# Decay attention with a mixture of experts on one core: constant rows by memsets, a new planned order, and transposes of the identity in TensorE's planned waits

## The chip, the cores and the metric

The kernel runs on one core of a Trainium2 chip. The metric is the device time of the whole program in microseconds (us), the median of three executions; lower is better. TensorE is called PE, VectorE DVE, ScalarE ACT, GpSimd POOL and SyncE SP, as in the profile.

## What is computed

For 8 batches and 8 heads of 576 rows with 64 columns each, in fp32, a causal attention whose scores carry a decay, and then a mixture of four experts over its output, each expert a causal attention of its own:

```python
scores = scale * (q @ k.T)
cum = cumsum(log(clip(f, 1e-4, 1)))
scores = where(causal, -1e9, scores + cum[:, None] - cum[None, :])
attn = softmax(scores) @ v                        # 8 batches x 8 heads
x = attn laid out as [8, 576, 512]
logits = x @ w_gate                               # 4 experts, the best 2 of each row count
for e in range(4):
    y = softmax(causal(scale * (x @ wq[e]) @ (x @ wk[e]).T)) @ (x @ wv[e]) @ wo[e]
    out += (weight of e in its row, 0 if not among the best 2) * y
```

## The kernel before

The work is cut into 48 units. A unit of kind a is two heads of one batch (4 for each batch, 32 in all); a unit of kind m is two experts of one batch (2 for each batch, 16 in all). The list `seq` starts with the four a units of batch 0; after that each batch's a units are followed by the m units of the batch before.

An a unit loads k and q of its two heads by four DMAs into a tile `nat` (L611, one of three buffers), turns them on PE (L624, 18 transposes of 64 columns, five chunks and then four, k on array rows 0 to 63 and q on rows 64 to 127), splits them into a rounded high part `kq` on ACT (L589) and a rest `ka` on DVE (L593), finds each row's maximum (PE L869, in the first two units also L872; DVE L888), turns the maxima (PE L925), copies them to `ms` (ACT L931) and moves them by DMA into one row of the tile `xa` (L399). The score matmuls (L965) end with one product of `xa` rows, which adds the decay and takes the maxima away. ACT makes the exponentials `P` (L976), POOL clears the diagonal (L982, L993), and PE multiplies with the values (L1038). DVE divides (L1085), PE turns the result back (L1101). From the third a unit on the maximum uses a table `tab` that POOL (L654) makes from the cumulated logs `cum`, which a DMA brings (L646). The m units project with the weights (L709, L827, L1165).

Tile `xa` (three buffers, 128 rows of 2 x 576 + 64 elements) holds per head, in rows 0 and 1 of its half, the two parts of the cumulated logs in the first 576 columns and constant -1 behind column 640; in row 63 the maxima, and -1 in the other columns of the first half. The function `consts` in `setup` fills it once: DVE or POOL writes -1 into the first 640 columns (L417), POOL zero into the others (L419), and then, for each half, the function `ones` issues a DMA (L424) that copies the -1 of rows 2 and 3 into rows 0 and 1 behind column 640. That is six DMAs in all. The rows of the cumulated logs come by L562 for the first unit and L568 for later ones.

What order the instructions have on each engine is worked out in Python while the kernel is built. Each piece of work is an `Op` with an engine, a key, a cost, the ops it depends on and the buffers it needs. `key` is the unit's number plus an offset by class of work (`PLAN`, by position in the batch, with `HEAD` and `TAIL` for the first and last four units). `Plan.run` goes through the ops by list scheduling: on each engine, among the ops that could start within `EPS` ns of the earliest one, that with the lowest key is taken. `Plan.start` says when an op can start by the model, `Plan.commit` books its cost: a PE op by its matmuls, a DMA by the time to issue it on SP, to land it and a `SLACK`. At the end every op's `emit` is called in the order of planned starts. Only the order reaches the chip; waits are real semaphores.

The planner's prices that the prediction uses: in `commit`, a DMA keeps SP for `issue` + 25 ns, goes at `t + issue + 450` or when the DMA before is through, takes `w` and lands `lat` later. In `dma`, a load of 576 packets of 256 bytes has `w` = 648 ns and `lat` = 1150 ns.

All loads and moves go through the one queue of SP.

Of the kernel before, what the change touches and what calls it, by code (L numbers as in the profile page):

```python
# [36 lines left out]
PLAN = dict(
    apply=((-3.69, -0.2), (1.91, 2.08), (-1.97, -2.51), (-2.59, -2.5), (2.97, 2.56), (-1.38, 0.57)),
    attend=((1.59, 6.1), (-1.72, 5.2), (1.87, 1.49), (1.87, 2.69), (2.89, 3.69), (2.85, 4.34)),
    cast=((-0.09, 1.61), (-1.47, 0.26), (-2.36, -1.76), (-2.3, -0.86), (-3.26, 1.5), (-6.95, -9.62)),  # L40
    front=((0.72, 3.77), (-4.95, 0.97), (-4.36, -7.02), (5.84, 9.48), (-1.56, 0.46), (-4.78, 0.96)),
    gate=((7.82, 17.49), (4.37, 7.38), (9.59, 17.28), (14.77, 14.75), (8.61, 13.31), (18.19, 18.71)),
    max=((-1.9, -1.68), (-3.57, -3.64), (-0.47, -0.46), (-1.25, -0.63), (-1.82, -0.88), (-1.83, -2.1)),
    mprep=((-5.49, -9.51), (-1.24, -8.56), (-2.91, -12.12), (-3.19, -8.05), (-3.1, -5.52), (-2.85, -5.41)),
    out=((12.37, 14.16), (-1.66, 5.19), (2.45, 9.19), (-5.4, 2.51), (1.88, 3.69), (5.94, 11.28)),
    prep=((-2.48, -0.56), (-2.12, -1.35), (-1.47, 0.32), (-1.82, -1.28), (-7.94, -3.61), (-8.41, -7.56)),
    rows=((-2.65, -6.62), (-11.0, -7.07), (-7.02, -3.23), (0.54, -3.2), (-6.33, -6.66), (-12.92, -13.93)),
    scores=((0.28, 0.67), (-1.44, -0.13), (-0.19, 0.25), (0.44, 0.37), (0.14, 0.03), (-0.76, 0.22)),
    sums=((-6.73, -12.09), (1.61, -9.24), (1.96, -8.53), (-4.38, -9.45), (-6.78, -10.99), (0.71, -7.59)),
    tabs=((5.21, -2.24), (1.53, -1.04), (6.91, 3.73), (5.35, -0.7), (4.67, 5.66), (-1.3, -5.57)),  # L50
    vals=((0.98, 0.65), (-0.3, -2.45), (-2.29, -5.3), (12.26, 9.3), (0.95, -0.58), (-7.18, -4.77)),
    weights=((6.93, 7.78), (16.12, 11.74), (9.43, 13.9), (4.47, 0.64), (15.35, 16.26), (9.04, 10.64)),
)
HEAD = dict(
    apply=(2.47, -1.78, -1.25, -2.7),
    attend=(-7.68, 3.1, -2.45, 6.22),
    cast=(-4.21, 0.81, 0.11, -0.52),
    front=(0.43, -1.73, 2.53, -4.04),
    gate=(0.37, -1.4, 0.8, -2.56),
    max=(-0.16, 0.86, -0.39, -1.35),  # L60
    mprep=(-2.19, -2.56, -2.41, 0.64),
    out=(-1.03, -4.48, -4.91, 0.66),
    prep=(-1.04, -0.44, -0.77, -1.26),
    rows=(-3.6, 3.37, -6.01, 0.74),
    scores=(0.31, 0.06, -0.21, -0.82),
    sums=(1.68, -3.76, 8.84, 0.33),
    tabs=(-2.41, 2.74, -1.74, 0.12),
    vals=(-0.52, 1.02, -3.29, -1.71),
    weights=(-0.08, 0.15, -5.46, -0.48),
)  # L70
TAIL = dict(
    apply=(-2.89, -2.65, 2.02, -6.52),
    attend=(3.47, 3.57, -4.81, 3.48),
    cast=(2.71, 0.37, 2.7, -1.07),
    front=(0.32, 1.1, -3.27, 0.54),
    gate=(-6.28, 1.66, -0.23, -2.38),
    max=(1.3, -3.61, -1.97, -1.97),
    mprep=(-2.15, -3.8, -7.38, 0.89),
    out=(-3.35, -4.26, 2.2, 1.98),
    prep=(0.41, -0.09, -0.26, -0.55),  # L80
    rows=(-0.23, 1.14, -2.46, -0.58),
    scores=(-2.96, -1.16, -0.35, 1.14),
    sums=(0.78, 4.91, -6.86, 2.75),
    tabs=(-0.79, -0.4, 2.07, 0.65),
    vals=(-3.77, -8.29, 4.81, 4.15),
    weights=(-6.29, -3.27, -0.84, 0.24),
)
# [53 lines left out]
class Plan:
# [1112 lines left out]
```

## Time and profile before

| | us |
|---|---|
| median of 3 runs | 670.53 |
| lowest and highest | 668.12, 671.59 |
| the profiled execution, its own time | 670.77 |
| the profiled execution, its span | 669.1 |
| PE busy in the span | 636.9 (95%) |
| DVE, ACT, POOL busy | 440.2, 333.6, 238.0 |

Times in views are us from the start of the span. The granted clock of PE is a share of full speed: 1.00 is 2.4 GHz, 0.50 is 1.2 GHz. A timeline's row is: start, duration of the run of equal instructions, engine, line, operation, out<-in, shape, count, and in brackets the idle time of the engine before it with what ended it. SPq stands for SP issuing DMAs: the duration is that of the issue, not of the transfer.

### The profile page before, as it was taken

The numbers are of one execution on the slowest core, as the hardware profiler recorded it, in microseconds if no ns is written. First come the engines' busy times: TensorE is split into PE (matmuls) and PEld (weight loads), VectorE is DVE, ScalarE is ACT, GpSimd is POOL, SyncE is SP. The second block draws the span as 40 slices with busy tenths as digits, with TensorE's granted clock in tenths as the row PEclk, the third lists the DMA queues.
The fourth block names the chain that finished last, engine by engine and source line by source line (L and its number), as shares of the span: only waits on it lengthen the run. The fifth ranks groups of instructions, "written<-read, shape, count | busy, mean of one in ns | idle before, by whom it ended". The sixth has DMA issues, their size and how long they took to land.

```text
span 669.1 us, 29785 instructions
## 1 busy us (share of the span) xinstructions
PE 636.9 (95%) x11928; PEld 611.5 (91%) x11928; DVE 440.2 (66%) x1889; ACT 333.6 (50%) x1092; POOL 238.0 (36%) x597
## 2 busy tenths in 40 slices
PE   3797899999999999999999999999999999999996
PEld 3586799989999999999999999999999999999995
DVE  4666467778578576776678775775677764753541
ACT  2443645564536643555436554566346544534543
POOL 6254566144324434144334434143332431100110
PEclk9887899999999999999999999999999999999999
DMA  4788686156412651256412662147622310001004
GB/s 99 139 170 166 135 157 132 47 128 107 87 38 67 169 122 40 54 119 170 102 38 58 147 134 57 40 102 175 112 58 55 105 38 21 3 18 65 3 6 140
DMA packets 136817, 60.62 MB, mean 91 GB/s; under 512 B 123260, under 2 KB 123740, under 8 KB 136680
## 3 DMA queue, kind: packets, MB, share of 16 engines
q1 hardware_dynamic: 136680, 58.73, 39.4%
q8 instruction: 93, 1.52, 1.0%
q14 instruction: 44, 0.36, 0.2%
HBM read 48.54 MB, written 9.88 MB: 87 GB/s over the span
## 4 chain that ended last, share of the span: by engine, by line
PE 80%; DMA 5%; ACT 4%; issue 4%; DVE 2%; POOL 2%; SPq 2%; POOLq 0%; ACTq 0%; DVEq 0%
PE ps L1038 22%; PE ps L965 20%; PE ps L827 15%; PE ps L709 9%; PE ps L869 5%; PE ps L1165 4%; DMA cum<-exn 2%; ACT P L976 2%; PE ps L624 2%; PE ps L1101 2%; DMA xa<-ms 1%; ACT xh L1137 1%; DMA out_dram<-outb 1%; DVE junk L888 1%; PE ps L925 1%
## 5 line engine op out<-in xcount | busy, mean ns | idle before, releaser
L976 ACT ACTIVATE P<-ps 128x320 f32<-128x320 f32 (+3 forms) x384 | 166.8, 492 | 36.8 <-PE ps L965 19.4
L654 POOL TENSOR_SCALAR_AFFINE_SELECT tab<-cum 128x192 f32<-128x192 f32 (+1 forms) x300 | 127.8, 452 | 75.5 <-DVE mxs L888 55.7
L888 DVE CUSTOM_DVE_ANT_0 junk<-ps,tab 128x64 bf16<-128x64 f32 (+2 forms) x300 | 119.6, 433 | 18.1 <-PE ps L869 10.8
L965 PE MATMUL ps<-kq,ka 64*128 64x320 f32 (+4 forms) x576 | 114.8, 323 | 1.2 <-DVE mxs L888 0.7
L593 DVE TENSOR_TENSOR ka<-ps,kq 128x320 fp32r<-128x320 f32 (+2 forms) x192 | 78.3, 451 | 53.3 <-ACT kq L589 53.1
L1038 PE MATMUL ps<-va,P 128*64 128x65 f32 x3400 | 111.5, 223 | 0.4 <-POOL tab L654 0.3
L1038 PEld LDWEIGHTS ps<-va,P 128*64 128x64 f32 x3400 | 106.9, 138 | 5.0 <-POOL tab L654 1.9
L965 PE MATMUL ps<-ka,kq 64*128 64x320 f32 (+4 forms) x576 | 106.7, 299 | 0.0
L965 PE MATMUL ps<-kq 64*128 64x320 f32 (+4 forms) x576 | 104.4, 297 | 0.2 <-issue 0.2
L982 POOL TENSOR_SCALAR_AFFINE_SELECT P<-P 128x256 f32<-128x256 f32 x96 | 39.1, 407 | 182.3 <-ACT P L976 172.9
L589 ACT ACTIVATE kq<-ps 128x320 fp32r<-128x320 f32 (+2 forms) x192 | 66.7, 411 | 60.6 <-PE ps L827 27.0
L993 POOL TENSOR_SCALAR_AFFINE_SELECT P<-P 128x256 f32<-128x256 f32 x96 | 39.0, 406 | 124.0 <-ACT P L976 120.3
L965 PEld LDWEIGHTS ps<-kq,ka 64*128 64x128 f32 (+1 forms) x576 | 73.5, 184 | 5.2 <-DVE mxs L888 1.5
L869 PE MATMUL ps<-kq 64*128 64x320 f32 (+4 forms) x576 | 75.7, 312 | 2.1 <-ACT kq L589 0.7
L965 PE MATMUL ps<-xa 64*128 64x320 f32 (+4 forms) x384 | 72.6, 302 | 4.9 <-DMA xa<-ms 4.9
L965 PEld LDWEIGHTS ps<-kq 64*128 64x128 f32 (+1 forms) x576 | 72.6, 183 | 0.7 <-issue 0.4
L965 PEld LDWEIGHTS ps<-ka,kq 64*128 64x128 f32 (+1 forms) x576 | 71.7, 183 | 0.2
L888 DVE CUSTOM_DVE_ANT_0 junk<-ps,mask 128x320 bf16<-128x320 f32 (+3 forms) x144 | 56.8, 420 | 16.8 <-ACT spot L546 8.1
L869 PEld LDWEIGHTS ps<-kq 64*128 64x128 f32 x576 | 56.7, 191 | 6.5 <-ACT kq L589 1.5
L965 PEld LDWEIGHTS ps<-xa 64*128 64x128 f32 (+1 forms) x384 | 52.1, 186 | 6.1 <-issue 4.3
L1065 DVE TENSOR_SCALAR rc<-ps 128x6 f32<-128x6 f32 x96 | 15.5, 162 | 57.5 <-PE ps L1038 57.5
L709 PE MATMUL ps<-vh,xh 64*128 64x260 f32 x320 | 52.7, 288 | 0.1
(127 smaller groups left out, 1553.2 us busy)
## 6 DMA issues: line engine op xcount, KB each, us to landing
cum<-exn SPq DMA_DIRECT2D x60, 288.0 KB
nat<-in_k_dram SPq DMA_DIRECT2D x64, 144.0 KB
nat<-in_q_dram SPq DMA_DIRECT2D x64, 144.0 KB
va<-in_v_dram SPq DMA_DIRECT2D x64, 128.0 KB
out_dram<-outb SPq DMA_DIRECT2D x24, 256.0 KB
out_dram<-nat SPq DMA_DIRECT2D x8, 256.0 KB
xa<-ms SPq DMA_DIRECT2D x64, 2.5 KB
va<-in_v_dram SPq DMA_DIRECT2D x32, 32.0 KB
```

The lines of the kernel that those rows point to most:

```text
L589: lambda: nc.scalar.activation(kqb.t[:, w, a:z], bank.t[:, :n], AF.Copy), [dep], [bank, kqb],
L593: lambda: nc.vector.tensor_tensor(kab.t[:, w, a:z], bank.t[:, :n], kqb.t[:, w, a:z].bitcast(F32), ALU.subtract),
L654: lambda cb=cb, tb=tb, i0=i0, o=o, n=n: nc.gpsimd.affine_select(tb.t[:, o : o + n], cb.t[:, :n], [[-1, n]], ALU.is_ge, NEG, base=i0, chann ...
L709: nc.tensor.matmul(banks[blk].t[:, :NV], xt[r, c0 : c0 + 128], (wl if i == 1 else wh)[r, c], start=(t == FIRST5[blk] and j == 0), stop=(j ...
L827: nc.tensor.matmul(banks[w][gg].t[:, :HS], (wl if i == 2 else wh)[r, c, es], x["l" if i == 1 else "h"][c].t[r, gg * HS : gg * HS + HS], st ...
L869: nc.tensor.matmul(banks[h].t[:, o:z], kf[:, S + i0 : S + i0 + 128], kf[:, j0 : j0 + n], start=True, stop=not decay)
L888: nc.vector.tensor_tensor_reduce(junk[turn[0] % 2][:, :n], bank.t[:, o:z], tab[h].t[:, at : at + n] if tab else mask[:, MW - n :], 1.0, lo ...
L965: nc.tensor.matmul(banks[h].t[:m, o:z], l, r, start=(i == 0), stop=(i == 3))
L976: lambda: nc.scalar.activation(pb.t[:, h, o : o + n], bank.t[:, :n], AF.Exp, scale=SCALE), [dep], [bank, pb],
L982: g.affine_select(pv, pv, [[0, 2], [1, 128]], ALU.is_ge, 0.0, base=0, channel_multiplier=-1)
L993: g.affine_select(pv, pv, [[0, 2], [1, 128]], ALU.is_ge, 0.0, base=0, channel_multiplier=-1)
L1038: nc.tensor.matmul(banks[s // 3].t[64 * c : 64 * c + 64, o : o + 65], lhs, vget(h, jb), start=jb == 0, stop=jb == t // 2)
```

## The change

1. The six DMAs of `ones` become six memsets of -1 on DVE, of two rows and 576 columns each, which wait for POOL's zeros in the same columns only.
2. All offsets in `PLAN`, `HEAD` and `TAIL` are new; a new table `SHIFT` adds an offset for each of the 48 units to each of the 15 classes. `EPS` shrinks on ACT, POOL and SP, `SLACK` grows a little, the planner's price for issuing a load becomes 650 ns for 576 packets, 1100 for 1024, 560 for 512 and 470 for others, where it was 510 for all. The memsets of `pads` get key 2.5 instead of 1.0.
3. Where a PE op takes a new PSUM bank, starts before 100 us of planned time and the plan has PE idle for more than 500 ns before it, `commit` notes a fill: (idle - 200) / 58 rounds of one transpose of the identity for each of at most two of the op's new banks. `run` emits them on PE ahead of the op. Nobody reads what they write; the op's own first product overwrites it. The plan's own times don't know of them.

```diff
+FILL_END = 100000.0
 PLAN = dict(
...
-    prep=((-2.48, -0.56), (-2.12, -1.35), (-1.47, 0.32), (-1.82, -1.28), (-7.94, -3.61), (-8.41, -7.56)),
+    prep=((-2.44, -1.72), (-2.13, -0.98), (-1.48, 0.24), (-1.72, -1.51), (-7.53, -4.49), (-7.25, -7.35)),
...
+SHIFT = dict(
...
-EPS = dict(PE=37.0, DVE=18.0, ACT=252.0, POOL=1439.0, SP=204539.0)
-SLACK = dict(PE=55.0, DMA=859.0, V=72.0)
+EPS = dict(PE=37.0, DVE=18.0, ACT=40.0, POOL=262.0, SP=1958.0)
+SLACK = dict(PE=59.0, DMA=1025.0, V=108.0)
...
     def commit(self, op, t):
         c = op.cost
+        new = [b for b in op.bufs if b.slot is None and b.ring is self.banks]
         for b in op.bufs:
             b.give()
         if op.eng == "PE":
             s = self.pe
+            idle = t - max(s["se"])
+            if new and t < FILL_END and idle > 500.0:
+                op.fill = int((idle - 200.0) / 58), new[:2]
...
         for _, _, op in sorted(order, key=lambda x: x[:2]):
+            if op.fill:
+                self.filler(*op.fill)
             op.emit()
...
-    issue, lat = dict(on=(640, 750), row=(730, 570), rows=(270, 1150), load=(510, 1150))[kind]
+    issue, lat = dict(on=(640, 750), row=(730, 570), rows=(270, 1150), load=(dict([(1024, 1100), (576, 650), (512, 560)]).get(packets, 470), 1150))[kind]
...
+    def filler(n, banks):
+        for _ in range(n):
+            for c, bank in enumerate(banks):
+                r = slice(64 * c, 64 * c + 64)
+                nc.tensor.transpose(bank.t[:, 0:64], ident[r], ident[r, r])
...
                 def ones(h):
-                    z = t[64 * h : 64 * h + 4].bitcast(F32)
-                    nc.sync.dma_start(z[0:2, S + GAP :], z[2:4, 0:S])
-
-                ready[kind, i] += [add("SP", a, dma(2, 2304, "rows"), lambda h=h: ones(h), [x, y]) for h in range(2)]
+                    vec.memset(t[64 * h : 64 * h + 2, S + GAP :].bitcast(F32), -1.0)
+
+                ready[kind, i] += [add("DVE", a, dict(ns=570.0, at=(0, 64 * h)), lambda h=h: ones(h), [y]) for h in range(2)]
...
-        ready["pads"] = add("POOL", 1.0, pool(0, 1900, False), pads)
+        ready["pads"] = add("POOL", 2.5, pool(0, 1900, False), pads)
```

## Rows read from the trace of the kernel before

**Rows 1.** The page, 40 slices of the span: PE busy and its granted clock, in tenths.
```profile
PE   3797899999999999999999999999999999999996
PEclk9887899999999999999999999999999999999999
```

**Rows 2.** Busy time by stretch: from:to, length, busy of five engines, clock, DMA share, GB/s.
```profile
0.00:100.00 100.00, 77.34 (x1240) 68.68 (x1240) 58.77 (x239) 44.11 (x132) 52.85 (x142) 0.90 0.74 144
...
27.90:38.00 10.10, 8.46 (x83) 7.59 (x85) 4.97 (x21) 4.09 (x13) 4.33 (x11) 0.50 1.17 194
51.90:58.80 6.90, 6.90 (x57) 6.73 (x59) 2.89 (x13) 3.61 (x13) 2.13 (x6) 0.52 0.84 191
69.40:72.10 2.70, 2.70 (x33) 2.66 (x32) 0.00 (x0) 1.49 (x4) 1.32 (x4) 0.50 0.96 255
100.00:656.00 556.00, 552.01 (x10633) 537.14 (x10634) 380.19 (x1647) 284.39 (x947) 185.16 (x456) 1.00 0.35 80
```

**Rows 3.** PE's waits in the first 100 us: total, times, longest.
```profile
PE ps L624 <- DMA nat<-in_k_dram: 8.3, 2, 7.7
PE ps L965 <- DMA xa<-ms: 4.9, 4, 4.0
```

**Rows 4.** Busy time by stretch again: two waits ahead of low clock, one dense part.
```profile
26.40:33.30 6.90, 4.06 (x36) 3.22 (x35) 3.14 (x13) 2.89 (x9) 3.01 (x8) 0.60 1.26 195
33.30:38.00 4.70, 4.70 (x50) 4.51 (x52) 1.83 (x9) 2.44 (x8) 2.62 (x7) 0.50 1.06 188
...
63.60:68.40 4.80, 0.51 (x3) 0.18 (x1) 1.19 (x5) 0.63 (x1) 1.18 (x1) 1.00 0.37 74
```

**Rows 5.** Timeline of PE: transposes at either clock, and the first unit's maximum.
```profile
10.26 1.22 PE L624 MATMUL ps<-ident,nat 64*128 64x64 f32 x17 [2.27 <-DMA nat<-in_q_dram]
11.81 0.53 PE L869 MATMUL ps<-kq 64*128 64x192 f32 x2 [0.33 <-ACT kq L589]
13.15 0.68 PE L872 MATMUL ps<-xa 63*128 63x192 f32 x2 [0.81 <-DVE ka L593]
...
18.98 0.25 PE L925 MATMUL ps<-ident,mxs 64*66 64x64 f32 x2 [1.31 <-DVE mxs L888]
...
158.15 0.67 PE L624 MATMUL ps<-ident,nat 64*128 64x64 f32 x16
```

**Rows 6.** Line L624 near 10 us and over the span: ns least/median/most, first and last start.
```profile
L624 PE MATMUL ps<-ident,nat x17: 311/312/366, 10.3 to 11.2; 64*128 64x64 f32 x17
...
L624 PE MATMUL ps<-ident,nat x576: 213/223/367, 7.7 to 542.0; 64*128 64x64 f32 x192
```

**Rows 7.** Timeline of POOL: the identity, and the last of three zero fills.
```profile
1.07 0.29 POOL L408 TENSOR_SCALAR_AFFINE_SELECT ident<-ident 128x128 f32<-128x128 f32 x1
...
7.15 0.58 POOL L419 MEMSET xa<- 128x576 f32 x1
```

**Rows 8.** Timeline of SP's issues from the start.
```profile
0.80 0.60 SPq L470 DMA_DIRECT2D P<-in_f_dram  x1
1.91 1.41 SPq L424 DMA_DIRECT2D xa<-xa  x2
...
6.16 1.37 SPq L611 DMA_DIRECT2D nat<-in_q_dram  x2
...
10.58 1.32 SPq L562 DMA_DIRECT2D xa<-tab  x2
```

**Rows 9.** Timeline of DVE: a memset, and the end of the cumulated logs.
```profile
1.66 0.54 DVE L471 MEMSET yn<- 64x576 f32 x1
...
7.15 0.75 DVE L489 SCALAR_TENSOR_TENSOR tab<-P,tab 64x576 fp32r<-64x576 f32 x1 [0.75 <-ACT tab L486]
```

**Rows 10.** Busy time by stretch again: ahead of and during the first maxima.
```profile
0.00:11.46 11.46, 1.53 (x18) 1.21 (x18) 3.96 (x5) 3.89 (x7) 9.97 (x46) 1.00 0.34 80
14.30:25.10 10.80, 8.98 (x102) 7.83 (x99) 10.52 (x48) 3.56 (x9) 0.00 (x0) 1.00 0.39 102
```

**Rows 11.** SP's issue of the maxima that PE waits for at 67.7.
```profile
65.80 1.54 SPq L399 DMA_DIRECT2D xa<-ms  x2
```

More of the change, by code (lines that the diff above doesn't have):

```diff
@@ L37 @@
 PLAN = dict(
[L38 to L42, printed above, removed]
@@ new lines @@
+    attend=((1.5, 6.04), (-3.87, 2.35), (1.89, 0.46), (1.82, 1.34), (2.92, 3.11), (2.97, 4.72)),
+    cast=((-0.89, -1.53), (-2.57, -0.25), (-2.57, -2.08), (-4.1, -3.26), (-3.19, -0.52), (-6.8, -9.1)),
+    front=((0.57, 0.89), (-1.33, 1.96), (-6.66, -6.99), (6.07, 5.44), (-1.49, -1.38), (-6.06, -1.53)),
+    gate=((4.75, 10.21), (1.82, 1.99), (13.48, 20.07), (15.22, 12.25), (7.03, 10.49), (22.98, 19.32)),
+    max=((-1.96, -1.18), (-3.09, -3.19), (-0.75, -0.65), (-1.29, -0.62), (-1.83, -0.92), (-1.83, -2.03)),
@@ new lines @@
+    mprep=((-4.93, -9.65), (-2.24, -10.49), (-2.15, -11.95), (-1.12, -9.8), (-4.53, -8.31), (-2.83, -7.07)),
+    out=((10.06, 10.93), (-0.88, 4.9), (4.73, 8.8), (-5.04, 4.17), (2.19, 2.95), (6.11, 10.73)),
+    prep=((-2.44, -1.72), (-2.13, -0.98), (-1.48, 0.24), (-1.72, -1.51), (-7.53, -4.49), (-7.25, -7.35)),
+    rows=((-2.97, -7.93), (-13.62, -9.5), (-5.74, -3.48), (0.64, -2.63), (-11.14, -9.78), (-14.39, -15.59)),
+    scores=((0.31, 0.85), (-1.77, -0.16), (-0.17, 0.19), (0.44, 0.2), (0.17, 0.03), (-0.86, 0.55)),
@@ L53 @@
+    sums=((-2.7, -8.75), (3.47, -6.61), (1.78, -8.66), (-2.85, -7.43), (-6.77, -12.99), (1.96, -4.37)),
+    tabs=((-2.08, -12.47), (-3.4, -7.88), (1.27, -4.07), (4.64, -5.39), (-2.53, -3.24), (-6.55, -13.95)),
+    vals=((0.35, -0.83), (-0.05, -4.74), (-2.59, -4.51), (15.44, 13.11), (-0.44, -2.23), (-8.26, -5.59)),
+    weights=((10.03, 8.54), (15.94, 10.69), (7.5, 8.21), (7.61, 0.32), (16.42, 14.24), (7.09, 8.25)),
 )
 HEAD = dict(
-    apply=(2.47, -1.78, -1.25, -2.7),
-    attend=(-7.68, 3.1, -2.45, 6.22),
@@ L57 @@
[L57 to L69, printed above, removed]
+    apply=(4.42, -2.47, -1.0, -2.74),
@@ new lines @@
+    attend=(-7.85, 2.03, -1.21, 6.69),
+    cast=(-4.22, -0.55, 0.51, -2.3),
+    front=(1.44, -0.45, 1.26, -2.94),
+    gate=(2.03, -0.47, 0.05, -2.08),
+    max=(-3.06, 2.56, -0.4, -2.78),
+    mprep=(-2.72, -3.38, -3.29, 0.27),
+    out=(-1.32, -2.44, -2.79, 0.51),
+    prep=(-0.3, -0.51, -1.01, -1.35),
+    rows=(-3.98, 5.02, -7.74, 1.31),
+    scores=(-0.2, 0.96, -0.41, 0.23),
+    sums=(1.05, -2.6, 9.31, -0.72),
+    tabs=(-3.76, 2.54, -1.73, 1.57),
+    vals=(-0.1, 1.22, -3.57, -4.07),
+    weights=(-0.59, 1.31, -5.31, 0.32),
@@ L70 @@
 )
 TAIL = dict(
[L72 to L84, printed above, removed]
@@ L85 @@
-    vals=(-3.77, -8.29, 4.81, 4.15),
-    weights=(-6.29, -3.27, -0.84, 0.24),
-)
-EPS = dict(PE=37.0, DVE=18.0, ACT=252.0, POOL=1439.0, SP=204539.0)
-SLACK = dict(PE=55.0, DMA=859.0, V=72.0)
+    apply=(-2.57, -4.59, 0.67, -4.81),
+    attend=(4.2, 3.74, -2.27, 0.83),
+    cast=(1.78, 0.16, 1.77, -1.66),
+    front=(0.15, 2.18, -3.21, 1.27),
+    gate=(-6.91, 4.29, -0.97, -0.75),
+    max=(1.49, -2.21, -1.87, -0.38),
+    mprep=(-1.66, -3.18, -5.14, 1.91),
+    out=(-2.41, -4.59, 2.32, 2.61),
@@ new lines @@
+    prep=(-0.1, 0.08, 1.42, 0.31),
+    rows=(1.64, 2.04, -1.56, -1.01),
+    scores=(-2.48, -1.95, 0.16, 1.03),
+    sums=(1.56, 6.27, -7.03, 3.28),
+    tabs=(-2.46, 0.85, 2.73, 1.18),
+    vals=(-1.99, -7.35, 3.39, 4.51),
+    weights=(-8.09, -4.62, -2.19, -1.6),
+)
+SHIFT = dict(
+    apply={0: -0.01, 1: -0.44, 2: -0.06, 3: 0.11, 4: 0.01, 5: 0.02, 6: -0.05, 7: -0.05, 8: 0.02, 9: 0.14, 10: -0.09,
[4 rows of a table added]
+    attend={0: -0.02, 1: 1.65, 2: 0.04, 3: 0.53, 4: 0.18, 5: 0.28, 6: -0.12, 7: 0.34, 8: 0.3, 9: 0.07, 10: 0.02, 11:
[4 rows of a table added]
+    cast={0: 0.12, 1: 0.05, 2: -0.05, 3: -0.47, 4: 0.05, 5: 0.11, 6: 0.22, 7: 1.41, 8: 1.45, 9: 3.37, 10: 3.68, 11:
[4 rows of a table added]
+    front={0: 0.6, 1: 0.08, 2: -0.27, 3: 0.08, 4: -0.63, 5: -0.68, 6: 0.42, 7: 0.97, 8: -0.01, 9: -0.48, 10: 0.62,
[4 rows of a table added]
+    gate={0: -0.37, 1: -0.28, 2: -0.36, 3: -0.66, 4: 0.1, 5: 0.56, 6: 0.23, 7: -0.12, 8: 1.25, 9: 0.58, 10: 0.7, 11:
[4 rows of a table added]
+    max={0: -0.08, 1: 0.15, 2: 0.09, 3: -0.06, 4: -0.2, 5: -1.04, 6: -0.4, 7: 0.03, 9: -0.03, 11: -1.04, 13: 0.06,
[3 rows of a table added]
+    mprep={0: -0.28, 1: -0.11, 2: -0.9, 3: -0.32, 4: -0.67, 5: -0.95, 6: -0.77, 7: -0.25, 8: 0.09, 9: -0.01, 10:
[4 rows of a table added]
+    out={1: 0.2, 2: -0.28, 3: 1.63, 4: 1.1, 5: 0.66, 6: 0.91, 7: -0.04, 8: -0.16, 9: 0.07, 10: -1.26, 11: -0.77, 12:
[4 rows of a table added]
+    prep={0: 0.36, 1: -0.09, 2: -0.23, 3: 0.01, 4: 0.03, 5: 0.01, 6: -0.08, 7: 0.96, 8: 1.52, 9: -0.86, 10: 0.08,
[4 rows of a table added]
+    rows={0: 0.04, 1: -0.2, 2: -0.75, 3: -1.54, 4: -1.32, 5: -0.91, 6: -0.35, 7: -0.15, 8: -0.67, 9: 0.68, 10: 0.79,
[4 rows of a table added]
+    scores={0: 0.01, 1: -0.32, 2: 0.01, 4: 0.02, 5: 0.19, 6: 0.04, 7: 0.03, 8: -0.02, 9: 0.01, 10: 0.33, 11: -0.03,
[4 rows of a table added]
+    sums={0: 0.52, 1: 0.13, 2: 0.06, 3: -0.23, 4: 1.3, 5: 0.97, 6: -0.38, 7: -0.61, 8: -0.06, 9: 0.58, 10: -0.5, 11:
[4 rows of a table added]
+    tabs={0: -0.14, 1: -0.47, 2: -0.63, 3: 0.79, 4: 2.52, 5: 2.07, 6: 0.54, 7: 1.76, 8: 0.2, 9: 0.86, 10: 0.18, 11:
[4 rows of a table added]
+    vals={1: 0.72, 3: -0.09, 4: 0.11, 5: -1.3, 7: 0.04, 8: -0.07, 9: 0.9, 10: 0.19, 11: -1.16, 12: -0.08, 13: 0.5,
[4 rows of a table added]
+    weights={0: 0.09, 1: -0.4, 2: 0.39, 3: 1.31, 4: 1.61, 5: 1.34, 6: 1.91, 7: -0.03, 8: -0.84, 9: -0.8, 10: 0.51,
[4 rows of a table added]
+)
@@ L132, in __init__ @@
         self.todo, self.next, self.rel, self.fin, self.pinned, self.can = 0, [], 0.0, None, False, 0.0
+        self.fill = None
         for d in deps:
@@ L385, in tile_decay_attention_moe @@
     add = plan.add
+    def filler(n, banks):
[3 more added lines that the diff above has]
+                nc.tensor.transpose(bank.t[:, 0:64], ident[r], ident[r, r])
+    plan.filler, plan.banks = filler, r_ps
     unit_no = [0]
@@ L394, in key @@
         move = HEAD[cls][i] if i < 4 else TAIL[cls][i - n_units + 4] if i >= n_units - 4 else 0.0
-        return i + a + (z - a) * frac + move
+        return i + a + (z - a) * frac + (move + SHIFT.get(cls, {}).get(i, 0.0))
     def copy_bits(dst, src):
```

10 lines of the change are left out of this document (1 added, 9 removed), and 59 rows, old and new, of tables (apply, attend, cast, front).

## Prediction

> **What bounds the kernel now.** I read the page's slices first. PE is busy nearly everywhere; only the first five slices, some 80 us, and the last one show larger gaps, and the granted clock is below full in the same early slices, and slightly in the last [rows 1]. Then busy time by stretch: from 100 to 656 us PE is busy 552.0 of 556 us at clock 1.00 [rows 2]. There a new order can win at most the 4.0 us that are idle and what denser packing saves, so the change must earn its time before 100 us, where PE is idle for 22.7 us (100 less 77.34 [rows 2]). PE's own waits say for whom: 8.3 us for the first loads of k, 4.9 us for the maxima, all of them DMAs [rows 3]. The second loss is the clock: three stretches ran at or near 0.50, that is 1.2 GHz: 27.9 to 38.0, 51.9 to 58.8 and 69.4 to 72.1 [rows 2]. Around the fall of the first PE had waited 2.8 us (6.90 less 4.06), ahead of the third 4.3 us (4.80 less 0.51) [rows 4]. Until about 19 us the clock's column says 1.00, but the instructions say half: 17 transposes took 1.22 us at 10.26, while 16 took 0.67 at 158.15 [rows 5].
>
> **The price of a filler.** Transposes overlap, so I take the pace between their starts. One alone lasts 0.31 us early and 0.22 late [rows 6], so (1.22 - 0.31)/16 = 57 ns each at the low clock and (0.67 - 0.22)/15 = 30 ns at the high one [rows 5]. A round of two is 114 ns low, 60 ns high. The plan sizes fillers with 58 ns: they fit at the high clock and last twice as long as planned at the low one.
>
> **The first filler** can be counted by hand from the planner's lines. SP takes f (470 + 25 ns) and four loads (650 + 25 each). The last starts at 495 + 3 x 675 = 2520, goes at 2520 + 650 + 450 = 3620 and lands at 3620 + 648 + 1150 = 5418, with SLACK 1025 at 6443. PE's latency of 45 gives a start at 6488 ns, and all before it is idle: (6488 - 200)/58 = 108 rounds. They need the identity, ready at 1.36 [rows 7], and start near 1.5. At the low clock throughout they last 108 x 114 = 12.3 us, to 13.8. If the first 2.7 us are low, like the shortest low stretch [rows 2], 24 rounds go low and 84 x 60 = 5.0 us high, to 9.2. If 8.7 us are low, as now from 10.26 to 18.98 [rows 5], 76 rounds go low and 32 high, to 12.1. I take 10.3, nearer the shorter case because the fillers leave no gaps, which the early work now has.
>
> **Constant rows by memsets.** SP loses six issues: 1.41 us for the first pair [rows 8], 1.31 for each of two more, 4.0 us in all. Two pairs stand ahead of q, and SP also waits from 1.40 to 1.91 before the first. Without them f, k and q follow one another: q is issued near 0.80 + 0.60 + 1.37 = 2.8 (k taken like q; with gaps 2.9) instead of 6.16, 3.3 us earlier, and lands near 6.9 instead of 10.2. But the first filler stands ahead of the transposes and ends at 10.3: that gain is blocked, and they start when they do now. What remains: the first unit's rows, issued at 10.58 though DVE had them at 7.90 [rows 8, 9], can go at 8.0, and the work behind the filler runs at the high clock. The first L872, now at 13.15, needs those rows and the way from the first transposes to L869, now 1.55 us (10.26 to 11.81 [rows 5]), an estimated 1.2 at the high clock: 11.6, 1.5 us earlier. DVE's maxima, which fill it from 14.3 to 25.1 (10.52 of 10.80 us [rows 10]), move with it. **Term 1: -1.5 us**, from -3.3 (nothing blocked) to +2.2 (filler to 13.8, then 1.55 as now: 15.35 against 13.15).
>
> For the six memsets the nearest row writes 64x576 in 0.54 us [rows 9]: 3.2 us on DVE, which has 11.46 - 3.96 = 7.5 us idle before 11.46 [rows 10]. They wait for POOL's zeros, the last of which end at 7.73 [rows 7], early enough: cost 0. Queued behind them on DVE are the logs' scan and the first split; a shift of half a us there is covered by the 2.7 us that the rows gain. If that cover fails and they fall into the full stretch, +3.2 at worst. The pads (14 small memsets) move behind the orders in POOL's queue; POOL is idle from 14.3 to 25.1 (0.00 [rows 10]) and their readers, the m units, come long after: 0, a cost only to the tables if they slid past 25.
>
> **The clock.** Where PE is dense, low clock costs half: 33.3 to 38.0 is 4.70 us at 0.50 [rows 4], so 2.35; 51.9 to 58.8 is 6.90 us busy of 6.90 [rows 2], so 3.4; 69.4 to 72.1 is 2.70, so 1.35. Together 7.1 us. The fillers stand where the plan sees waits over 0.5 us, which aren't quite those of the chip, so I take nearly two thirds. **Term 2: -4.5**, from -7.1 to 0. The Trainium skill, "TensorE: Matmul & The Clock Gate", Part 4, says that transposes don't count as busy for this clock in the way matmuls do. No run here shows it, for the trace has no stretch of transposes alone longer than 18 instructions; by that rule term 2 would be 0 and the first rival below would hold.
>
> **The order.** The waits within 26.4 to 33.3 (2.8 us) and 63.6 to 68.4 (4.3 us) [rows 4] end with loads or maxima that came late from SP's queue; the maxima of 67.7 were issued at 65.80 [rows 11], behind values. The new plan prices a load of 576 packets at 650 ns, where the rows show 1.37 us for two [rows 8] and 510 was written. On SP it takes what is ready within 2 us rather than by key alone, and SP has 4.0 us less to issue. I take half of 7.1. **Term 3: -3.5**, from -7.1 to 0. Past 100 us the order can lose as well as win: 0, with half of the idle 4.0 us as the bound either way.
>
> **Later fillers.** Each stands in PE's queue ahead of an op, and all behind that op waits with it. A filler whose wait isn't real costs its own length, and one whose bank was only just released can't start before the op itself could. About 10 of the 22.7 idle us lie before 10.26; some 12.7 are left. If the plan keeps 6 us of such waits and a quarter is late: **Term 4: +1.5**, from 0 to +6 (all late, high clock).
>
> **Sum.** -1.5 - 4.5 - 3.5 + 1.5 = -8.0. The profiled execution took 670.77 us (span 669.1 and 1.7 around it), 0.24 above the median of 670.53: 662.8 by the one, 662.5 by the other, which I take.
>
> **Rivals.**
> *The fillers don't lift the clock (slower).* Every round costs 114 ns. The first filler ends at 13.8: term 1 is +2.2. The 6 us planned later last 12 and end 6 late: term 4 is +6. Term 2 is 0, the order's -3.5 stays: +4.7, 675.2. It decides when late fillers cost more than the order gives, 3.5 us. For it: a round puts only one pass of 64 columns on each half of the array. Against: the trace has transposes among other work at either level, so nothing in it sets them apart.
> *The whole prize.* All of 7.1 and 7.1, term 1 as it is, no late filler: -15.7, 654.8. For it: the early waits are mostly for DMAs, and SP is what is relieved. Against: DVE is full from 14.3 to 25.1 and isn't hurried.
> *The gains cancel.* The new order moves waits to other buffers, tables or values, and late fillers take what the clock gives: terms 1 and 2 as above, term 3 at 0, term 4 at +6: 670.5. A slip of 1 us repeated in each of eight batches gives about the same from the forecast.
>
> **How the numbers follow.** A measurement of this kernel can tell about 0.5%, 3.4 us. Forecast (658 to 667): 0.50. Whole prize (below 658): 0.20. Cancel (667 to 674): 0.15. Slower (above 674): 0.15. Faster is the first two, 0.70. For 8 in 10 I leave out the far ends: 651 to 673.
>
> **What would show it.** SP's first rows: f, k, q without L424, q issued near 3. PE busy from 1.5 with transposes of `ident` by `ident`, and the first L624 on `nat` at 10.3 (13.8 would be the first rival). No 0.50 between 28 and 72. PE's waits for `xa<-ms` below 2 us. From 100 us on the same work per us. I am wrong if L872 comes after 13.2, if 0.50 follows fillers, or if PE idles for tables or values where it idled for maxima.

## The result and the profile after

The changed kernel takes **661.78 us** (median of 6 runs, 659.81 to 662.61), the kernel before took 671.48 beside it (668.12 to 676.09): ratio 0.9846, 95% interval 0.9807 to 0.9886. It is 10 us faster, where 8.0 were forecast. The forecast of 662.5 is met within 1 us, but not for the reasons that its sum gives: the term for the order was three times too small, and the terms for the memsets, the clock and the fillers together, put at -4.5, brought almost nothing.

I read after in the order of the prediction. First the slices of the page: the low digits of the start are gone in both lines [rows 1].

```profile
PE   8999999999999999999999999999999999999996
PEclk9999999989999999999999999999999999999998
```

Then busy time by stretch (from:to, length, busy of PE, PE's weight loads, DVE, ACT and POOL with counts, clock, DMA share, GB/s). The three stretches that ran near 0.50 [rows 2] run at 1.00, and from 100 to 656 us the engines do the same work:

```profile
0.00:100.00 100.00, 94.93 (x2035) 88.00 (x2037) 67.93 (x269) 48.63 (x147) 59.08 (x153) 1.00 0.84 163
...
27.90:38.00 10.10, 9.38 (x183) 8.20 (x181) 7.25 (x34) 6.75 (x19) 6.06 (x15) 1.00 1.09 180
51.90:58.80 6.90, 6.62 (x112) 5.83 (x109) 3.82 (x17) 5.14 (x17) 4.01 (x10) 1.00 0.89 143
69.40:72.10 2.70, 2.70 (x47) 2.40 (x43) 2.20 (x12) 2.70 (x9) 2.04 (x6) 1.00 1.01 214
100.00:656.00 556.00, 552.80 (x10564) 534.45 (x10561) 376.34 (x1629) 283.38 (x944) 178.96 (x446) 1.00 0.32 78
```

That looks like the forecast come true. But a busy PE is no proof here, because the fillers (L476) are themselves PE work. They have to be taken off. The same view of the first 82 us, of all instructions and then of L476 alone:

```profile
0.00:82.00 82.00, 77.11 (x1664) 71.04 (x1664) 57.05 (x222) 39.55 (x120) 48.47 (x134) 1.00 0.85 159
...
0.00:82.00 82.00, 28.88 (x668) 25.81 (x668) 1.00 0.85 159
```

Of 1664 PE instructions 668 are fillers: 996 belong to the kernel. Before did 808 in that time (its row stands with the first experiment). A count of real instructions begun by 82 us is the measure for the rest of this text. It is a rough one: it comes from one profiled execution of each kernel, and instructions differ in length. From 100 to 656 us before began 10633 in 556 us [rows 2], one in 52 ns, so 188 more of them are worth 9.8 us.

The first filler is close to the hand count: 217 transposes from 1.43 to 10.12, where 108 rounds to 10.3 were forecast. But the timeline of PE shows that three more runs of filler transposes (64, 28 and 39) stand between the first unit's transposes and its maximum:

```profile
1.43 8.69 PE L476 MATMUL ps<-ident 64*128 64x64 f32 x217 [1.43 <-POOL ident L501]
...
10.00 0.68 PE L716 MATMUL ps<-ident,nat 64*128 64x64 f32 x16
...
10.57 2.19 PE L476 MATMUL ps<-ident 64*128 64x64 f32 x64
...
13.22 1.05 PE L476 MATMUL ps<-ident 64*128 64x64 f32 x28
14.54 1.42 PE L476 MATMUL ps<-ident 64*128 64x64 f32 x39 [0.28 <-issue]
...
15.94 0.28 PE L964 MATMUL ps<-xa 63*128 63x192 f32 x2
```

L964 (L872 before) comes at 15.94, where 11.6 was forecast and before had 13.15 [rows 5]: 2.8 us later than before, and yet the kernel is 10 us faster.

### The profile page after: what moved, and what is told of

The parts are those of the page before. It is cut to its first block, busy times and chain, and to the rows that moved or that the text cites. A ratio compares the mean times of both kernels' runs of the same rounds, so it can differ in the third digit from the quotient of the medians.

```text
span 660.8 us, 31111 instructions
## 1 busy us (share of the span) xinstructions
PE 647.7 (98%) x12596; PEld 622.4 (94%) x12596; DVE 444.3 (67%) x1895; ACT 333.2 (50%) x1092; POOL 238.0 (36%) x597
## 4 chain that ended last, share of the span: by engine, by line
PE 83%; DVE 4%; issue 4%; ACT 4%; DMA 2%; POOL 1%; SPq 1%; POOLq 0%; ACTq 0%; DVEq 0%
PE ps L1130 20%; PE ps L1057 19%; PE ps L919 15%; PE ps L801 9%; PE ps L1257 7%; PE ps L961 6%; PE ps L476 3%; PE ps L716 3%; ACT P L1068 2%; DVE junk L980 2%; PE ps L1193 2%; DMA outb<-in_moe_wv_dram 1%; POOL tab L746 1%; DVE ka L685 1%; DMA out_dram<-outb 1%
## 5 line engine op out<-in xcount | busy, mean ns | idle before, releaser
L746 POOL TENSOR_SCALAR_AFFINE_SELECT tab<-cum 128x192 f32<-128x192 f32 x300 | 127.6, 452 | 93.9 <-DVE mxs L980 64.1
L1057 PE MATMUL ps<-kq,ka 64*128 64x320 f32 (+4 forms) x576 | 105.7, 315 | 1.1 <-DVE xl L1232 0.6
L1057 PE MATMUL ps<-ka,kq 64*128 64x320 f32 (+4 forms) x576 | 99.8, 292 | 0.0
L1057 PE MATMUL ps<-kq 64*128 64x320 f32 (+4 forms) x576 | 98.5, 292 | 0.0
L961 PE MATMUL ps<-kq 64*128 64x320 f32 (+4 forms) x576 | 76.2, 309 | 0.8 <-ACT pl L1095 0.2
L1057 PEld LDWEIGHTS ps<-kq,ka 64*128 64x128 f32 (+1 forms) x576 | 67.3, 179 | 3.5 <-DVE xl L1232 0.8
L1057 PEld LDWEIGHTS ps<-kq 64*128 64x128 f32 (+1 forms) x576 | 66.7, 178 | 0.2
L1057 PEld LDWEIGHTS ps<-ka,kq 64*128 64x128 f32 (+1 forms) x576 | 65.9, 178 | 0.3 <-issue 0.2
L1057 PE MATMUL ps<-xa 64*128 64x320 f32 (+4 forms) x384 | 66.2, 291 | 0.0
L801 PE MATMUL ps<-vh,xl 64*128 64x260 f32 x320 | 52.2, 279 | 0.0
L801 PE MATMUL ps<-vl,xh 64*128 64x260 f32 x320 | 52.1, 279 | 0.0
```

The source lines that it names most:

```text
L746: lambda cb=cb, tb=tb, i0=i0, o=o, n=n: nc.gpsimd.affine_select(tb.t[:, o : o + n], cb.t[:, :n], [[-1, n]], ALU.is_ge, NEG, base=i0, chann ...
L801: nc.tensor.matmul(banks[blk].t[:, :NV], xt[r, c0 : c0 + 128], (wl if i == 1 else wh)[r, c], start=(t == FIRST5[blk] and j == 0), stop=(j ...
L961: nc.tensor.matmul(banks[h].t[:, o:z], kf[:, S + i0 : S + i0 + 128], kf[:, j0 : j0 + n], start=True, stop=not decay)
L1057: nc.tensor.matmul(banks[h].t[:m, o:z], l, r, start=(i == 0), stop=(i == 3))
```

## The experiments

Each kernel was timed in 5 rounds beside the kernel before, in three groups. In the first (no fillers, memsets or fillers in the old order, the new order with DMAs and fillers) before took 671.8 us; in the second (the new order alone, loads behind the maxima, prices alone, memsets behind the logs) 672.6; in the third (first filler, later fillers, memsets behind the logs with fillers) 672.2. Kernels of different groups are compared by their ratio to before; I call 672 x (1 - ratio) the gain. That of the change is 10.3.

### Which of the three parts gains

**The fillers off.**

```diff
-FILL_END = 100000.0
+FILL_END = 0.0
```

> The changed kernel without any filler; order, memsets and all else kept. Clock theory (the fillers hold the clock at 2.4 GHz and that is where most of the gain is): stretches at 0.50 come back between 20 and 75 us and the time rises by 4 us or more, to 666 or above. Order theory (the gain comes from maxima that no longer wait behind loads; the fillers change little or cost as much as they give): 660 to 664, and the first maximum starts about 3 us earlier than the 15.8 us it has with fillers.

Measured: 660.97, ratio 0.9836 (0.9811 to 0.9861), gain 11.0. Without a single filler the kernel is as fast. Busy time by stretch, before and then this kernel:

```profile
0.00:82.00 82.00, 59.45 (x808) 51.90 (x810) 47.69 (x195) 34.25 (x102) 40.10 (x119) 0.88 0.72 141
```

```profile
0.00:82.00 82.00, 67.18 (x1006) 59.77 (x1008) 57.30 (x224) 41.27 (x125) 49.06 (x136) 0.96 0.85 164
0.00:100.00 100.00, 85.18 (x1383) 77.20 (x1385) 68.88 (x275) 50.38 (x151) 60.05 (x155) 0.97 0.82 163
```

By the clock's column, before ran its first 100 us at 0.90 [rows 2] and this one at 0.97. That isn't a comparison. In every trace of this case the column says 1.00 from the start to the first change that it shows, while single transposes of 64 columns take 311 ns, the value of 1.2 GHz [rows 6]; the prediction noted this of before, up to 19 us. So the start has to be read from the instructions. The transposes that begin from 22 to 29.5 us (ns least/median/most, first and last start), of this kernel and then of after:

```profile
L716 PE MATMUL ps<-ident,nat x18: 305/311/366, 22.7 to 26.1; 64*128 64x64 f32 x18
...
L716 PE MATMUL ps<-ident,nat x18: 222/222/225, 25.7 to 29.0; 64*128 64x64 f32 x18
```

Without fillers PE is at 1.2 GHz up to 26.1 us at least (the next transposes, from 33.1, take 223); with them it is at 2.4 GHz there. So the fillers do lift the clock of the start, and yet the kernel with them is no faster. What the order gains in waits is read below, from the order alone.

**The memsets alone, in the old order**, at the places where the DMAs were.

```diff
-                    z = t[64 * h : 64 * h + 4].bitcast(F32)
-                    nc.sync.dma_start(z[0:2, S + GAP :], z[2:4, 0:S])
+                    vec.memset(t[64 * h : 64 * h + 2, S + GAP :].bitcast(F32), -1.0)
```

> The kernel before with its own order, where only the six DMAs of the constant rows are memsets, issued at the same places of the order. Queue theory (six issues less on SP move the whole head): 667 or below, q issued near 3 and the first transposes near 7. Order theory: the wait of 4 us for the maxima near 64 stays, since its place in SP's order stays; 669 to 672.

Measured: 671.81 (12 runs), ratio 1.0005 (0.9986 to 1.0025): nothing, with 824 instructions by 82 us. What the start gains doesn't last to the end; PE's wait for the maxima, for one, grew. PE's waits in the first 100 us (total, times, longest), against 4.9, 4 and 4.0 before [rows 3]:

```profile
PE ps L964 <- DMA xa<-ms: 5.7, 2, 5.1
```

**The fillers alone, in the old order**: the lines of the change that make them, added to before. They give 16 fillers.

```diff
+            if new and t < FILL_END and idle > 500.0:
+                op.fill = int((idle - 200.0) / 58), new[:2]
...
+            if op.fill:
+                self.filler(*op.fill)
             op.emit()
```

> The kernel before with its own order and its DMAs, and fillers where its own plan has TensorE wait (16 fillers, the first of 134 rounds). Clock theory: no stretch at 0.50, about 4 us faster than before, 666 to 667. Order theory: the wait near 64 stays and the clock's gain is lost again in it, 669 to 672.

Measured: 676.2, ratio 1.0069 (1.0042 to 1.0095): 4.6 us slower, with 771 real instructions by 82 us. The place of the old wait, in the timeline of PE:

```profile
70.50 1.33 PE L982 MATMUL ps<-xa 64*128 64x320 f32 x2 [5.58 <-DMA xa<-ms]
```

No filler stands there, and the longest wait stays, longer than before (5.58 against 4.02 us). The fillers sit where the plan has gaps, not where the chip has them. How the 4.6 us divide between this wait and the fillers' own length isn't shown.

**The new order with the DMAs in place of the memsets**, fillers on, and then off as well, which leaves the new order alone (with it the keys of the pads and the plan's prices).

```diff
-                    vec.memset(t[64 * h : 64 * h + 2, S + GAP :].bitcast(F32), -1.0)
+                    z = t[64 * h : 64 * h + 4].bitcast(F32)
+                    nc.sync.dma_start(z[0:2, S + GAP :], z[2:4, 0:S])
```

> The changed kernel with the same order and fillers, where the six memsets are the DMAs of before again, issued at the same places of the order. Queue theory: about 3 us slower than the changed kernel, 664 to 666. Order theory: within 1.5 us of it, as the cumulated logs are late there for the memsets as well.

> The new order alone: the changed kernel without fillers and with the constant rows by DMAs at the same places of the order. If the order is all of the gain and the memsets only matter beside fillers: 660 to 662, as without fillers. If the memsets are worth the 4.3 us that they are with fillers: 664.5 to 666.

Measured: 666.05 with fillers, ratio 0.9907 (0.9880 to 0.9933), gain 6.2; 662.14 without, ratio 0.9855 (0.9825 to 0.9884), gain 9.7. **The order alone is nearly the whole change.** Its own rows show where it works, before first, then the new order alone:

```profile
0.00:40.00 40.00, 24.20 (x288) 21.03 (x290) 21.85 (x83) 15.09 (x40) 18.97 (x70) 0.87 0.68 130
40.00:82.00 42.00, 35.25 (x528) 30.88 (x525) 25.84 (x113) 19.15 (x62) 21.12 (x50) 0.88 0.75 151
```

```profile
0.00:40.00 40.00, 24.53 (x306) 21.58 (x306) 25.57 (x94) 15.40 (x40) 20.49 (x73) 1.00 0.77 153
40.00:82.00 42.00, 38.67 (x661) 34.65 (x659) 26.71 (x115) 22.50 (x75) 26.69 (x60) 0.92 0.77 161
```

Up to 40 us PE does about the same (306 instructions to 288). The column's 1.00 there isn't the clock, for the transposes take 312 ns up to 28.0. From 40 to 82 us PE does 661 instructions where it did 528, in 3.4 us more of busy time. The gain is in the middle of the head, not at its start. The transposes from 22 to 29.5 us, and the first line of the page:

```profile
L717 PE MATMUL ps<-ident,nat x18: 305/312/367, 25.7 to 28.0; 64*128 64x64 f32 x18
...
PE 635.5 (96%) x11928; PEld 609.3 (92%) x11928; DVE 441.7 (67%) x1889; ACT 333.2 (50%) x1092; POOL 237.5 (36%) x597
```

The page tells what the order wins. Its span is 662.0 us, so PE is idle for 26.5 us of it; before PE was idle for 32.2 (669.1 less 636.9). So 5.7 of the 7.1 us by which this span is shorter are waits that are gone, 3.8 of them before 100 us (PE is busy 81.09 us there, 77.34 before [rows 2]). Only 1.4 us are busy time, which is where a better clock would show.

### What the order mends

In before, ACT copied a set of maxima at 57.47, and SP issued them at 65.80 [rows 11]. Timelines of before, of ACT, of SP and of PE:

```profile
57.47 0.32 ACT L931 ACTIVATE ms<-ps 10x64 fp32r<-10x64 f32 x2 [0.88 <-PE ps L965]
...
57.10 2.67 SPq L533 DMA_DIRECT2D outb<-in_moe_wv_dram  x2
59.81 2.54 SPq L672 DMA_DIRECT2D va<-in_v_dram  x3
62.40 0.73 SPq L679 DMA_DIRECT2D va<-in_v_dram  x1
...
67.74 0.38 PE L965 MATMUL ps<-xa 64*128 64x320 f32 x1 [4.02 <-DMA xa<-ms]
```

A pair of small moves stood 8 us, from the end of the copy to the issue, behind loads of weights and values that could wait, as the next experiment shows. The new order alone issues its maxima of that time 3 to 5 us after the copy (copies at 53.30 and 62.97, issues at 58.36 and 65.92), and PE's wait for them falls to 0.7 us.

**Only this place mended, in the old order**: eight loads of SP (two of weights, six of values), with what hangs on them, are emitted behind that pair of maxima.

```diff
+        sp = [op for op in ops if op.eng == "SP"]
+        last, held = sp[85], sp[74:82]
...
+            if last is not None and (op in held or any(op in x.next for x in held)):
...
+                late.append(op)
+                continue
             op.emit()
+            if op is last:
...
+                for x in late:
+                    x.emit()
```

> The kernel before with one change of its order: the eight loads (two of weights, six of values) that SP issues from 57.1 to 64.9 us stand behind the two DMAs of the maxima that it issued at 65.8. Theory, maxima behind loads: TensorE's wait of 4 us near 64 and the low clock after it are gone and the time falls by 4 to 6 us, to 666 to 668. Rival, the wait only moves, since the loads are late in their turn: 670 to 672.

Measured: 669.59 (12 runs), ratio 0.9952 (0.9929 to 0.9975), gain 3.2, with 887 instructions by 82 us. SP's timeline, then PE's waits from 0 to 100, then a stretch:

```profile
57.87 1.54 SPq L412 DMA_DIRECT2D xa<-ms  x2
59.46 1.05 SPq L546 DMA_DIRECT2D outb<-in_moe_wv_dram  x2
```

```profile
PE ps L978 <- DMA xa<-ms: 0.5, 2, 0.3
PE ps L978 <- ACT ms L944: 1.9, 1, 1.9
```

```profile
65.00:70.00 5.00, 4.34 (x59) 4.34 (x61) 0.94 (x3) 4.05 (x15) 1.98 (x5) 0.66 0.72 201
```

The maxima are issued at 57.87, 0.9 us behind the end of ACT's copy (56.95 here), and the wait of 4.9 is 0.5. So this blockage is real and is shown to cost about 3 us (1.7 to 4.8 by the interval); 1.9 of its wait comes back as a wait for ACT, and the clock is low in another place (0.66 from 65 to 70). The other 6.5 us of the order's gain have no such single place that I isolated.

**The new prices alone**, with the old offsets: the planner's line for loads is changed, and the plan made anew.

```diff
-    issue, lat = dict(..., load=(510, 1150))[kind]
+    issue, lat = dict(..., load=(dict([(1024, 1100), (576, 650), (512, 560)]).get(packets, 470), 1150))[kind]
```

> The kernel before, where only the planner's prices for issuing loads are the new ones, and the order is planned anew by the old offsets. If the old order was bad because it took loads to be cheaper on SP than they are: 665 to 669, with the wait for the maxima near 64 shorter than 2 us. If the new offsets are what counts: 670 to 673.

Measured: 687.93, ratio 1.0223 (1.0189 to 1.0256): 15 us slower. By 82 us it is level with before (811); it loses behind, where before has no idle time (39.89 busy of 40 at clock 1.00 in the same stretch):

```profile
85.00:125.00 40.00, 35.33 (x603) 32.10 (x600) 18.30 (x81) 13.68 (x43) 21.49 (x41) 0.83 0.64 141
```

So truer prices by themselves don't make a better order. The new offsets under the old prices weren't run, so how the two share the gain is open.

### What the fillers cost

**The first filler only**, and **the 16 later ones only**, both in the changed kernel:

```diff
-FILL_END = 100000.0
+FILL_END = 7000.0
```

```diff
-            if new and t < FILL_END and idle > 500.0:
+            if new and 7000.0 < t < FILL_END and idle > 500.0:
```

> The changed kernel with its first filler alone (109 rounds), none of the sixteen later ones. If the first filler is what delays the start and the later ones pay it back: 662 to 664. If it costs nothing at the end, because the head has slack for it: 660 to 662.

> The changed kernel with the sixteen later fillers alone. If they hold the clock for a gain that the first one spoils: 658 to 660. If their lateness takes what the clock gives: 660.5 to 663.

Measured: 659.17 with the first alone, ratio 0.9802 (0.9781 to 0.9823), gain 13.3; 663.2 with the later ones alone, ratio 0.9866 (0.9844 to 0.9888), gain 9.0. Against none at all (gain 11.0), the later ones cost 2.0; added to the first (13.3 to 10.3), they cost 3.0. Side by side, the first alone is 4.0 us faster than the later ones alone, and that is clear of the intervals. The pairs with and without the later fillers overlap in theirs; that they cost something rests on three such pairs that agree (a third follows below). The first filler costs nothing, and may gain 1 to 2 us; the intervals of the kernels with and without it overlap too, so I leave that open.

How a later filler costs is seen in the timeline of PE, of after and, in the last row, of the kernel with the first filler alone. It writes the bank of the op behind it, so it can't start before that bank is released, and the op, whose wait ended with the same release, then waits for the filler:

```profile
27.24 1.76 PE L476 MATMUL ps<-ident 64*128 64x64 f32 x49 [0.58 <-DVE ka L685]
28.80 0.45 PE L716 MATMUL ps<-ident,nat 64*128 64x64 f32 x8
...
26.09 0.69 PE L716 MATMUL ps<-ident,nat 64*128 64x64 f32 x7 [0.87 <-DVE ka L685]
```

In the last row the transposes start when DVE's `ka` ends; in after the filler starts then, and the transposes come 1.56 us later. Six fillers of after that start with the end of a wait, at 18.07, 22.11, 27.24, 36.27, 46.75 and 57.51, last 6.3 us together (1.02 + 0.59 + 1.76 + 1.03 + 1.34 + 0.52).

What the clock is worth by itself these runs don't show. With the first filler alone PE is at 2.4 GHz for the first transposes and low behind them. Its transposes from 10 to 16 us, and then a stretch:

```profile
L716 PE MATMUL ps<-ident,nat x37: 221/222/273, 10.3 to 15.5; 64*128 64x64 f32 x37
...
17.60:33.00 15.40, 13.90 (x124) 11.95 (x124) 11.55 (x51) 8.06 (x23) 7.81 (x20) 0.60 0.89 179
```

The kernel without fillers is low from its first transposes on (311 ns up to 26.1, above). So the first filler gives some more time at 2.4 GHz, and this kernel gains 13.3 where none gains 11.0. That would fit a small price of low clock, but the filler also moves the first unit's transposes (17 of 18 begin at 7.57 without it) to 10.3 us, and the intervals overlap.

### What the memsets cost

In after the memsets stand in DVE's queue ahead of the logs' last step (L581), and two of them wait for POOL's zeros. Timeline of DVE, and SP's issue of the logs' rows:

```profile
4.11 0.54 DVE L516 MEMSET xa<- 2x576 f32 x1 [0.61 <-POOL xa L512]
...
8.21 0.54 DVE L516 MEMSET xa<- 2x576 f32 x1 [1.09 <-POOL xa L512]
...
9.48 0.75 DVE L581 SCALAR_TENSOR_TENSOR tab<-P,tab 64x576 fp32r<-64x576 f32 x1
...
10.31 1.43 SPq L654 DMA_DIRECT2D xa<-tab  x2
```

The logs end at 10.23, where before had 7.90 [rows 9]: 2.3 us late. **The memsets of the second and third buffer emitted behind L581**, without fillers:

```diff
-                def ones(h):
+                def put(h):
                     vec.memset(t[64 * h : 64 * h + 2, S + GAP :].bitcast(F32), -1.0)
...
+                def ones(h):
+                    if i == 0 or "done" in late:
+                        put(h)
+                    else:
+                        late.append(lambda h=h: put(h))
...
+            for x in late:
+                x()
+            late.append("done")
```

> The changed kernel without fillers, and with the memsets for the second and third tile behind the cumulated logs on DVE. Theory, the memsets hold up the logs by 2.3 us because they wait for POOL: the logs end near 7.9 instead of 10.2, the first unit's rows go out some 1.3 us earlier, and what of that lasts to the end makes 659 to 660.5. Rival, the head has slack there: 661 as without this.

Measured: **658.91**, ratio 0.9799 (0.9771 to 0.9826), gain 13.5, the fastest kernel of all, 2.5 us more than with the memsets ahead. Timelines of DVE, SP and PE (the last two rows are of PE in the kernel with no fillers and the memsets ahead), then the first 82 us by stretch:

```profile
7.15 0.75 DVE L588 SCALAR_TENSOR_TENSOR tab<-P,tab 64x576 fp32r<-64x576 f32 x1 [0.75 <-ACT tab L586]
...
9.08 1.43 SPq L663 DMA_DIRECT2D xa<-tab  x2
...
12.89 0.62 PE L973 MATMUL ps<-xa 63*128 63x192 f32 x2 [0.64 <-DMA xa<-tab]
...
24.54 0.93 PE L1066 MATMUL ps<-kq,ka 64*128 64x192 f32 x2
...
12.45 0.90 PE L964 MATMUL ps<-xa 63*128 63x192 f32 x2 [0.29 <-DMA xa<-tab]
...
26.16 0.92 PE L1057 MATMUL ps<-kq,ka 64*128 64x192 f32 x2
```

```profile
0.00:82.00 82.00, 65.77 (x1030) 58.19 (x1030) 58.78 (x232) 42.22 (x129) 49.21 (x138) 1.00 0.87 166
```

The logs end at 7.90 again and their rows leave 1.2 us earlier. But the first maximum doesn't start earlier for it (12.89 against 12.45); PE is 1.6 us ahead only at the first scores (24.54 against 26.16). How much of the gain is the logs' isn't shown, for the clock differs too. The column's 1.00 hides a low start here as well (the transposes from 22.3 to 24.5 take 312 ns), but behind it no stretch is low, while the kernel with the memsets ahead shows 0.66 from 45 to 50 and from 65 to 70. By the pages both do the same 11928 PE instructions, in 631.9 us busy here and 636.7 there, and wait about as long (23.8 and 22.9 us idle). So in these two executions, of which this one is the fastest of its six, the 3.9 us between the spans are busy time, as a clock that is low for less time would make it.

**The same with the 16 later fillers, and with all 17 at half length** (in the second, 58 becomes 116):

```diff
-FILL_END = 0.0
+FILL_END = 100000.0
...
-            if new and t < FILL_END and idle > 500.0:
+            if new and 7000.0 < t < FILL_END and idle > 500.0:
```

```diff
-FILL_END = 0.0
+FILL_END = 100000.0
...
-                op.fill = int((idle - 200.0) / 58), new[:2]
+                op.fill = int((idle - 200.0) / 116), new[:2]
```

> The kernel with the memsets of the second and third tile behind the logs (658.9 without fillers), now with the sixteen later fillers. Its clock without fillers was 0.998, so there is little for them to give: 659 to 662, slower by as much as they are late. If the clock at the start still matters: below 658.

> The same with all seventeen fillers at half their length, so that the first ends near 6.5 us, ahead of q, and TensorE is at 2.4 GHz from its first real work. If low clock in the first 25 us costs anything at the end: 656 to 658. If DVE and the DMAs set the pace there: 658.5 to 660.5.

Measured: 660.9, ratio 0.9837 (0.9814 to 0.9861), gain 11.0, and 660.6, ratio 0.9826 (0.9803 to 0.9849), gain 11.7. Later fillers cost 2.5 here, in line with the 2.0 and 3.0 above; halved, and with the first, all of them cost 1.8. The halved ones did lift the start, as meant (the transposes from 7.2 to 18.4 take 222 to 223 ns at the median), and the kernel is no faster for it; since the later halves stand in it too, that doesn't price the clock alone. With later fillers in both, the memsets behind L581 gain 2.3 us over those ahead (660.9 against 663.2, beside the same runs of before).

### All kernels side by side

Real PE instructions begun by 82 us (fillers taken off), what 52 ns for each one more than 808 would give, and the gain measured:

| kernel | instructions | at 52 ns, us | gain, us |
|---|---|---|---|
| prices alone | 811 | 0.2 | -15.0 |
| fillers, old order | 771 | -1.9 | -4.6 |
| memsets, old order | 824 | 0.8 | -0.3 |
| loads behind the maxima, old order | 887 | 4.1 | 3.2 |
| new order, DMAs, fillers | 937 | 6.7 | 6.2 |
| later fillers only | 962 | 8.0 | 9.0 |
| new order alone | 963 | 8.1 | 9.7 |
| after | 996 | 9.8 | 10.3 |
| no fillers | 1006 | 10.3 | 11.0 |
| memsets behind, later fillers | 984 | 9.2 | 11.0 |
| memsets behind, half fillers | 1004 | 10.2 | 11.7 |
| first filler only | 998 | 9.9 | 13.3 |
| memsets behind, no fillers | 1030 | 11.5 | 13.5 |

In all but the first row the count follows the gain, within 3.4 us. So far as this rough count goes, the gains are made or lost before 82 us; the first row is the one that loses behind.

## Why the prediction was right, and where its steps were wrong

**What bounds the kernel** was read rightly. The dense part neither gained nor lost (552.80 of 556 us busy, 552.0 before [rows 2]), and the change lives before 100 us.

**Term 3, the order (-3.5, bound -7.1): mis-sized.** It measured -9.7 by itself, beyond the bound. The step that failed took half of two waits, of 2.8 and 4.3 us [rows 4]; the order gave as much as the whole of both and more. Its trace (an execution of 663.75 us, slower than its median, so that it has 7.1 of the 9.7) shows 5.7 us less of PE's waits and 1.4 less busy time than before's. So the order is paid in waits, and hardly in clock: its start is low up to 28.0 at least, where before shows low clock up to about 19 us and again from 27.9 [rows 2]. Which waits they are, beyond the one for the maxima, isn't isolated. The mechanism named, maxima behind values on SP, was right, and mending it alone brought 3.2.

**Term 2, the clock by fillers (-4.5, bounds -7.1 and 0): the mechanism right, no gain behind it.** The three low stretches vanished, and most of the low start with them (222 ns in after where the kernel without fillers has 311). But that kernel is as fast, and in the old order the fillers made it slower. Terms 2 and 4 together forecast -3.0; all fillers together measured +0.7 (gain 10.3 against 11.0), which isn't clear of nothing. So either low clock was priced too high (half of each dense stretch, as if PE were last wherever it is busy) or lateness too low. Which of the two stays open, since no run here lifts the clock without moving work as well.

**Term 1, memsets and start (-1.5): sign roughly right, way wrong.** SP's part came as told: q issued at 2.86 (2.9 forecast). Two things were missed. The fillers behind the first (64, 28 and 39 transposes) weren't counted by hand, so L964 came at 15.94, against 12.45 without fillers. That is past 13.2, which the prediction named as a sign of being wrong. And for the six memsets the queue of DVE was seen, but what it shifts was put at half a us: "early enough" looked at the end of POOL's last zeros, while DVE waits for the zero fills with the logs queued behind it, and they end 2.3 us late. The cover that I named, the early rows, was just what they took away: rows issued at 10.31, not at 8.0. Measured with fillers, memsets against DMAs bring 4.1 (gain 10.3 against 6.2), without fillers 1.3 (not clear of the intervals), in the old order nothing. That they are worth more with fillers may be because q comes before the filler ends; that is argued, not shown.

**Term 4, later fillers (+1.5, bounds 0 and +6): right in mechanism, somewhat small.** 2.0 to 3.0 measured, net of what their clock gave. That a filler on a just-released bank can't start before the op itself was the step, and its rows show it.

**The sum.** -1.5 - 4.5 + 1.5 = -4.5 was forecast for all that isn't order; the new order alone takes 662.14 and the change 661.78, so it was -0.4 (-0.6 by the ratios). -3.5 for the order was -9.7. Two errors of 4 and 6 us nearly cancel; the median was met by luck as much as by reading.

**The rivals.** "The fillers don't lift the clock" is refuted in its mechanism. Rows of L476 in after, of two stretches (ns least/median/most, first and last start):

```profile
L476 PE MATMUL ps<-ident x8: 311/311/311, 4.8 to 5.1; 64*128 64x64 f32 x8
...
L476 PE MATMUL ps<-ident x20: 221/223/304, 5.3 to 6.0; 64*128 64x64 f32 x20
```

PE had done nothing but transposes since 1.43, and one falls from 311 to 223 ns between 5.1 and 6.0, the two values of [rows 6]. So these transposes lift the granted clock, against what the Trainium skill, "TensorE: Matmul & The Clock Gate", Part 4, says of transpose mode; the measurement decides. The rows call them MATMUL, and whether that mode was on no row shows. (Before had 27 transposes in a row too, from 73.10, not 18 at most as the prediction says; PE was at 2.4 GHz by then, so they tell nothing.) Net of the fillers' lateness it was worth nothing that these runs can measure. The rival that the gains cancel is true of the fillers and memsets together, which add 0.6 to the order's 9.7, not of the order. The whole prize, 654.8, wasn't reached by any kernel; 658.91 is the nearest.

## What to carry to other kernels

Read the clock of a kernel's start from the length of equal instructions, not from a column that may say 1.00 there, before you credit a gain to it or deny it one. Mend what PE waits for first: the order did so and gained 9.7 us at a clock that stayed low at the start. Keep PE busy with dummy work only where it can't stand ahead of real work: not on a bank that the next op needs, and not by a plan that doesn't know where the chip waits. A cheap instruction moved to an idle engine costs what it waits for in that engine's order, so put it behind whatever the critical chain has queued there.
